# One buffer per PSUM bank, fillers only at the start, and a new step order in a fused attention and MLP kernel

## The chip, the cores and the metric

The kernel runs on one core of one Trainium2 chip. The time is device microseconds of one execution of the whole program; several executions are timed, and their median is compared. One more execution is recorded by the hardware profiler, and its span, from the first to the last instruction, is what the profile's shares refer to. The core has a matrix engine (TensorE, called PE, with its weight loads shown apart as PEld), three engines that work on whole tiles (VectorE or DVE, ScalarE or ACT, GpSimd or POOL), a fifth that here only issues transfers (SyncE or SP), and 16 DMA engines. Each engine takes its instructions strictly in the order in which the program gives them to it. PE's results go to PSUM, which has eight banks of 128 partitions by 512 fp32 values; DVE and ACT read them from there, POOL can't.

## The reference

Two stages follow one another: a linear attention with decay in blocks of 64 positions, and an MLP with the activation h + sin(alpha h)^2 / alpha. `q`, `k`, `v` are (4, 8, 768, 64), the MLP has 3072 tokens, 512 inputs and outputs and 2048 inner features.

```
for b in range(nb):
    intra = einsum('bhic,bhjc->bhij', qb, kb) * Dmask
    intra = einsum('bhij,bhjd->bhid', intra, vb)
    inter = einsum('bhid,bhde->bhie', qb * lam_pow, kv_state)
    out[:, :, sl] = intra + inter
    kv_state = lam_block * kv_state + einsum('bhsd,bhse->bhde', kb * rev_pow, vb)
x = out.transpose(0, 2, 1, 3).reshape(B * S, H * D)
h = x @ w_in
s = sin(alpha * h)
g = h + s * s / (alpha + 1e-09)
return (g @ w_out).astype(float32)
```

## The kernel before, in words

**Units.** The attention is cut into 24 units: 256 positions (two chunks of 128) of four heads of one batch element. For a unit `u`, SP loads three fp32 tiles (`ld{u}q`, `ld{u}k`, `ld{u}v`, line 694). `cq` and `ck` cast q and k to bf16 (line 706, on ACT, POOL or DVE), `sv` scales v by the decay (POOL, line 721). q and k are turned: for units 0 to 8 by PE (`tq`, `tk`, tile `pt`, line 729) with an eviction by ACT or DVE (`e0`, `e1`), for units 9 to 23 by a DMA that SP issues (`dt`, line 746). `sc` computes the scores into the tile `sp` (line 752), `mm` masks them (DVE, line 765). `kv` computes the unit's addition to the state (tile `kp`, in later units a part of `okv`, line 778); from it `bx` or `d0`, `d1` and `n0`, `n1` make the decayed state `kvbd` and what is carried on (DVE for units 3 to 7, else POOL, with an ACT copy `kva` ahead; lines 799 to 859). `in` and `io` multiply q by the state and the masked scores by v, both into `okv` (lines 864 and 875), and `oe` writes the unit's output, scaled, to the tile `xt` (DVE, line 894). From unit 8 on, `sc`, `kv` and the previous unit's `in` and `io` are one PE step, `step{u}`.

**Groups.** Four units make a group of 512 tokens; there are six. For each group, 16 steps `f1_g_f` multiply `xt` by 128 columns of `w_in` (four matmuls into the tile `hps`, line 911); ACT takes the sine (`sn`), ACT or POOL squares it (`sq`), DVE adds (`g`, into the tile `gall`). An `f1` step of a group needs all four of its units; only the first feature block of group 0 is done in two halves of two units each. Then four token tiles of 128 are multiplied by `w_out`, each in four quarters of four matmuls, `f2_g_m_j` (line 939), evicted by ACT (`ev`) and stored by SP (`out`). The weights are loaded and cast by POOL's DMA queue, `w_in` in four pieces `wi0` to `wi3` (256, 512, 512 and 768 columns), `w_out` in four equal ones `wo0` to `wo3`. A piece may be issued only after a named `sv` step (`WG` and `WH`, lines 538 and 539). The first load of unit 5 waits until the piece that holds feature block 4 of `w_out`, `wo1`, has landed (`GATES`, line 521), and SP takes its other instructions in order behind it.

**PSUM.** Four banks, `f0` to `f3`, hold `pt`, `kp`, `hps`, `ops` and a few tables, handed out by the planner; two banks hold `sp` and two hold `okv`. `bank()` (line 572) makes a new tile, with a name and shape of its own, under the bank's tag each time. The framework sets every semaphore wait; a tile under the same tag as an older one waits for all that used the older one.

**The order.** All steps are `Op` objects with a cost, the steps they come after, the buffers they take and give back, and a due time `vt`. `Plan.run` plays through the kernel with these costs: whenever an engine is free, it takes of the steps that are ready and whose buffers are free the one with the lowest due time. What comes out is only an order; each engine then runs its steps in it. `TUNE` adds a number to a step's due time and may pin the step to one engine. The due times without it are 32 per group and 8 per unit (`vt_unit`, line 1023, is 32 g - 40 + 8 r + u for unit u = 4 g + r up to unit 7); pieces of the weights have -700 plus their place among the eight.

**Fillers.** Nine matmuls of 512 columns and 60 of 256, `warm` with the tile `bz`, multiply constants into a free `f` bank and nobody reads them (lines 986 and 1012). In the plan each of the 60 takes 0.11 us and comes `FLAG` = 0.03 us or more after the one before. Their due times are 2,000,000 and up.

```
for i in range(NFILL):
    dop = add("warm", on("PE", 0.11), [dop], 2e6 + i, dummy, take=("f",), mode="n", lag=FLAG)
    dop.give, dop.part = ((dop, "f"),), 2
```

**What the plan knows of DMA.** `BEGIN` is how long after its issue a transfer starts, `FETCH` lists times at which transfers are slowed for `HOLD` = 1.5 us, `SHARE` is the rate that is left to them.

Of the kernel before, what the change touches and what calls it, by code (L numbers as in the profile page):

```python
# [12 lines left out]
FP32 = mybir.dt.float32  # L13
# [17 lines left out]
class Plan:  # L31
# [3 lines left out]
    BEGIN, LAND, DEPTH = {"SP": 0.4, "POOL": 2.4}, 1.3, 6  # L35
    HEAD = 0.75
    FETCH = (4.0, 14.5, 21.5, 27, 48, 56, 66.5, 76.5, 86, 98.5, 108.5, 121, 131.5, 142.5, 157)
    HOLD, SHARE = 1.5, 0.35
# [129 lines left out]
def kernel(  # L168
# [27 lines left out]
        "lam": (0.0, 'ACT'), "iden": (0.0, 'POOL'), "lamb": (0.0, 'PE'), "tabc": (0.0, 'DVE'),  # L196
        "tab1": (1.2, 'POOL'), "tabm": (852.8, 'DVE'), "tabi": (-21.2, 'POOL'),
        "tabd": (-499.1, 'POOL'), "tab2": (-428.0, 'DVE'), "tab0": (-2.1, 'PE'),
        "tab4": (-818.2, 'DVE'), "tab3": (-962.3, 'ACT'), "alq": (0.0, 'ACT'),
# [301 lines left out]
    WI = (256, 512, 512, 768)  # L501
    WO = (4, 4, 4, 4)
    HALVES = ()
    NWARM = 9
    NLAM = 2
    NFILL = 60
    FLAG = .03
    DMAT = {9, 10, 11, 12, 13, 14, 15, 16, 17, 18, 19, 20, 21, 22, 23}
    NH0 = 1
    H0 = 24  # L510
    NX = False
    UV = 0
    UE = 1
# [834 lines left out]
```

## Time and profile before

| | us |
|---|---|
| runs | 221.74, 220.77, 221.69 (median 221.69) |
| span of the profiled execution | 218.2 |
| PE busy, of the span | 211.9 |
| of it `f1` matmuls (`hps`, 388) | 91.9 |
| of it `f2` matmuls (`ops`, 368) | 83.1 |
| ACT, POOL, DVE busy | 141.3, 124.6, 121.0 |
| first `f1` half block starts | 19.02 |
| first `f1` block of group 1 starts | 57.62 |
| last matmul of `f2` ends, about | 214.1 |

The span is split over 40 slices of 5.45 us; in each, the page gives the busy share in tenths (9 is 90% or more) for each engine, the clock that PE was granted, and what DMA moved:

```profile
PE   8999999999999999999999999999999999999994
ACT  3454699656499664878968787476778695634220
POOL 7959599768989899999898755611101100001000
PEclk9999999999999999999999999999999999999999
GB/s 148 302 287 146 192 206 207 240 292 247 264 240 209 217 263 268 240 175 235 301 152 224 267 58 99 0 51 0 50 48 0 51 50 24 60 11 74 27 141 98
```

PE is shown as busy from the first slice to the last, POOL up to about 130 us, and DMA carries most of its bytes before 130 us. A busy figure doesn't tell work from filler. In the list of waits, each line has the engine and line that waited, what it waited for, and then the total in us, the number of times and the longest. In a timeline row come start, duration, engine, line, operation, tile written and tiles read, shape and count; in brackets the idle time ahead of it and what ended it ("issue" means that it waited for nothing that the profile shows). A row that stands for several instructions runs from the first one's start to the last one's end.

### The profile page before, as it was taken

What the parts mean: (1) busy time and instruction counts of PE and PEld (TensorE: products, weight loads), DVE (VectorE), ACT (ScalarE), POOL (GpSimd) and SP (SyncE); (2) the same over time, 40 slices, a digit from 0 to 9 for tenths busy, and PEclk for the clock granted to TensorE, in tenths of its full rate; (3) what the DMA queues carried; (4) which work ended last, traced back from release to release, by engine and by line L of the source; (5) the groups of instructions that cost most, each with busy time, mean ns of one, the idle gap of its engine ahead of it and who ended that gap; (6) DMA issues with size and microseconds to landing.
All of it is one profiled execution on the core that took longest, in us unless ns stands there. A gap on an engine that the chain in (4) does not pass through costs nothing.

```text
span 218.2 us, 5305 instructions
## 1 busy us (share of the span) xinstructions
PE 211.9 (97%) x2102; PEld 108.3 (50%) x2102; DVE 121.0 (55%) x176; ACT 141.3 (65%) x252; POOL 124.6 (57%) x209
## 2 busy tenths in 40 slices
PE   8999999999999999999999999999999999999994
PEld 3556644455544555545654545554444444444463
DVE  3457676457368974657794797975345451311100
ACT  3454699656499664878968787476778695634220
POOL 7959599768989899999898755611101100001000
PEclk9999999999999999999999999999999999999999
DMA  5999999898999999969999964020220221203164
GB/s 148 302 287 146 192 206 207 240 292 247 264 240 209 217 263 268 240 175 235 301 152 224 267 58 99 0 51 0 50 48 0 51 50 24 60 11 74 27 141 98
DMA packets 62139, 33.65 MB, mean 154 GB/s; under 512 B 17938, under 2 KB 59170, under 8 KB 62114
## 3 DMA queue, kind: packets, MB, share of 16 engines
q1 hardware_dynamic: 57776, 29.04, 59.5%
q0 software_dynamic: 4224, 4.19, 12.0%
q8 instruction: 16, 0.26, 0.5%
q10 hardware_dynamic: 114, 0.07, 0.1%
q14 instruction: 9, 0.07, 0.1%
HBM read 27.27 MB, written 6.29 MB: 154 GB/s over the span
## 4 chain that ended last, share of the span: by engine, by line
PE 90%; POOL 4%; issue 2%; ACT 1%; DVE 1%; POOLq 0%; ACTq 0%
PE hps L916 35%; PE ops L952 33%; PE bz L989 6%; PE sp L759 3%; PE okv L952 3%; PE okv L882 2%; PE pt L735 2%; PE okv L869 2%; PE okv L793 1%; POOL vb L725 1%; POOL kvs L859 1%; POOL qk L719 1%; PE kp L793 1%; DVE gall L935 1%; ACT s L923 1%
## 5 line engine op out<-in xcount | busy, mean ns | idle before, releaser
L935 DVE SCALAR_TENSOR_TENSOR gall<-s,r_sb,hps 128x512 bf16<-128x512 bf16 (+1 forms) x97 | 69.8, 740 | 63.7 <-ACT s L930 47.8
L916 PE MATMUL hps<-xt,w_in_sb 128*128 128x512 bf16 (+1 forms) x388 | 91.9, 377 | 1.4 <-DVE gall L935 0.8
L952 PE MATMUL ops<-w_out_sb,gall 128*128 128x512 bf16 (+1 forms) x368 | 83.1, 370 | 0.0
L923 ACT ACTIVATE s<-hps,alpha_sb 128x512 bf16<-128x512 f32 (+1 forms) x97 | 65.4, 679 | 25.9 <-PE hps L916 24.7
L952 PEld LDWEIGHTS <-gall 128*128 128x128 bf16 x400 | 38.5, 98 | 41.7
L916 PEld LDWEIGHTS <-w_in_sb 128*128 128x128 bf16 x388 | 36.5, 98 | 43.2 <-issue 2.6
L932 POOL TENSOR_TENSOR s<-s 128x512 bf16<-128x512 bf16 x21 | 21.9, 1041 | 51.9 <-ACT s L923 51.9
L930 ACT ACTIVATE s<-s 128x512 bf16<-128x512 bf16 (+1 forms) x76 | 46.6, 623 | 1.7
L767 DVE TENSOR_TENSOR sm<-sp,mask 128x1024 bf16<-128x1024 f32 x24 | 29.3, 1220 | 4.6 <-PE sp L759 4.5
L725 POOL TENSOR_TENSOR vb<-st_v,R 128x512 bf16<-128x512 f32 x24 | 25.0, 1045 | 2.5 <-DMA st_v<-in_v_dram 2.5
L958 ACT COPY ob<-ops 128x512 f32<-128x512 f32 x21 | 12.3, 584 | 20.2 <-PE ops L952 20.2
L821 POOL TENSOR_TENSOR kvbd<-kvx,LBD 128x256 bf16<-128x256 f32 x32 | 19.7, 614 | 2.5
L818 POOL TENSOR_TENSOR kvx<-kva,kvs 128x128 f32<-128x128 f32 x32 | 14.6, 456 | 7.8 <-ACT kva L803 7.7
L901 DVE TENSOR_TENSOR xt<-okv,ET 128x512 bf16<-128x512 f32 x24 | 16.5, 686 | 3.1 <-PE okv L882 2.8
L989 PE MATMUL bz<-const-bfloat16-1.0 128*128 128x256 bf16 (+1 forms) x69 | 16.4, 311 | 1.5 <-PEq L1332 0.8
L719 POOL CAST qk<-st_q 128x512 bf16<-128x512 f32 x19 | 11.5, 612 | 2.5 <-PE okv L793 2.5
L719 POOL CAST qk<-st_k 128x512 bf16<-128x512 f32 x17 | 10.4, 613 | 0.8 <-DMA st_k<-in_k_dram 0.8
L759 PE MATMUL sp<-qt 64*64 64x128 bf16 x384 | 10.0, 221 | 0.0
L882 PE MATMUL okv<-sm,vb 64*64 64x128 bf16 x384 | 9.7, 218 | 0.0
L859 POOL TENSOR_TENSOR kvs<-kvx,ET 128x128 f32<-128x128 f32 x24 | 9.4, 403 | 0.0
L803 ACT COPY kva<-okv 128x256 f32<-128x256 f32 (+1 forms) x16 | 5.0, 314 | 6.6 <-PE okv L793 6.4
L742 ACT COPY qt<-pt 128x512 bf16<-128x512 bf16 x9 | 5.2, 590 | 6.2 <-PE pt L735 6.2
(63 smaller groups left out, 110.7 us busy)
## 6 DMA issues: line engine op xcount, KB each, us to landing
st_q<-in_q_dram SPq DMA_DIRECT2D x24, 256.0 KB, 5.1
st_k<-in_k_dram SPq DMA_DIRECT2D x24, 256.0 KB, 5.3
st_v<-in_v_dram SPq DMA_DIRECT2D x24, 256.0 KB, 5.0
out_dram<-ob SPq DMA_DIRECT2D x46, 128.0 KB, 2.5
w_out_sb<-in_moe_w_out_dram POOLq DMA_DIRECT2D x4, 512.0 KB, 11.9
w_in_sb<-in_moe_w_in_dram POOLq DMA_DIRECT2D x2, 512.0 KB, 6.4
w_in_sb<-in_moe_w_in_dram POOLq DMA_DIRECT2D x1, 768.0 KB, 9.6
w_in_sb<-in_moe_w_in_dram POOLq DMA_DIRECT2D x1, 256.0 KB, 6.4
```

The costliest lines, as they stand in the source:

```text
L719: ENGINE[op.eng].tensor_copy(out=o, in_=i)
L725: ENGINE[op.eng].tensor_tensor(out=T[u, "vb"][:], in0=T[u, "v"][:].rearrange("p h two e -> p two h e"), in1=R[:, :, hs].unsqueeze(3).to_br ...
L759: nc.tensor.matmul(out=T[u, "sp"][half[c], hd, par, hp, :], lhsT=QT[half[hd], 1, par, hp, half[c]], rhs=QT[half[hd], 0, :, hp, half[c]], s ...
L767: V.tensor_tensor(out=T[u, "sm"][:].rearrange("p hd par hp i -> p (hd par) hp i"), in0=T[u, "sp"][:].rearrange("p hd par hp i -> p (hd par ...
L821: G.tensor_tensor(out=bd[:], in0=X.unsqueeze(2).to_broadcast([P, 2, 2, D]), in1=LBD[:, hs, :].unsqueeze(3).to_broadcast([P, 2, 2, D]), op= ...
L916: op.ins = nc.tensor.matmul(out=op.tile[:, cols], lhsT=w_in_sb[:, c, f * P:(f + 1) * P], rhs=xt[g][:, c].rearrange("p b c i -> p (b c i)") ...
L923: A.activation(out=op.tile[:, cols], in_=mm.tile[:, cols], func=ACTF.Sin, scale=alpha_sb[:, f:f + 1])
L930: A.activation(out=op.tile[:, cols], in_=s1, func=ACTF.Square)
L932: ENGINE[op.eng].tensor_tensor(out=op.tile[:, cols], in0=s1, in1=s1, op=ALU.mult)
L935: V.scalar_tensor_tensor(out=gall[g][:, f, cols], in0=sq.tile[:, cols], scalar=r_sb[:, f:f + 1], in1=mm.tile[:, cols], op0=ALU.mult, op1=A ...
L952: op.ins = nc.tensor.matmul(out=first.tile[:, cols], lhsT=gall[g][:, f, m * P:(m + 1) * P], rhs=w_out_sb[:, f, cols], start=(f == 0), stop ...
L989: nc.tensor.matmul(out=bz[:, :w], lhsT=nc.const_aps.tensor(1.0, [P, P], BF16), rhs=nc.const_aps.tensor(1.0, [P, w], BF16), start=True, sto ...
```

## The change

Four things change. `bank()` makes one tile per `f` bank for the whole kernel, when the bank is first used, and returns a view of it in the shape and type asked for. Fillers are planned as before, with `FLAG` 0.2 instead of 0.03, and those that the plan starts at 40 us or later are not emitted. Three of the planner's DMA figures are new. Every number in `TUNE` is new (949 entries each), and most pins are gone: before, all but 21 entries named an engine, after, 46 do, among them the evictions, casts and squares of the early units and groups.

```diff
-    BEGIN, LAND, DEPTH = {"SP": 0.4, "POOL": 2.4}, 1.3, 6
+    BEGIN, LAND, DEPTH = {"SP": 0.4, "POOL": 1.9}, 1.3, 6
     HEAD = 0.75
-    FETCH = (4.0, 14.5, 21.5, 27, 48, 56, 66.5, 76.5, 86, 98.5, 108.5, 121, 131.5, 142.5, 157)
-    HOLD, SHARE = 1.5, 0.35
+    FETCH = (4.0, 21.5, 48, 56, 66.5, 76.5, 86, 98.5, 108.5, 121, 131.5, 142.5, 157)
+    HOLD, SHARE = 1.5, 0.6
...
-        "n12": (-186.7, 'POOL'), "in2": (2000055.6, 'PE'), "io2": (2000064.6, 'PE'),
-        "oe2": (-8.6, 'DVE'), "cq3": (24.5, 'POOL'), "ck3": (0.0, None), "sv3": (-5.1, 'POOL'),
...
-        "sc3": (2000052.1, 'PE'), "kv3": (2000051.2, 'PE'), "mm3": (-71.1, 'DVE'),
...
-        "n13": (-0.3, 'POOL'), "in3": (0.0, 'PE'), "io3": (2000059.7, 'PE'), "oe3": (-891.7, 'DVE'),
...
-        "in4": (-69.2, 'PE'), "io4": (29.2, 'PE'), "oe4": (0.0, 'DVE'), "cq5": (70.3, 'ACT'),
-        "ck5": (-287.2, 'ACT'), "sv5": (118.3, 'POOL'), "tq5": (-92.8, 'PE'), "e05": (68.8, None),
...
-        "oe5": (5.3, 'DVE'), "cq6": (0.0, 'ACT'), "ck6": (32.1, 'POOL'), "sv6": (-90.1, 'POOL'),
...
-        "oe7": (96.4, 'DVE'), "wi0": (-221.9, 'POOL'), "wi1": (679.4, 'POOL'), "wi2": (-215.8, 'POOL'),
-        "wi3": (-216.7, 'POOL'), "wo0": (15.7, 'POOL'), "wo1": (641.9, 'POOL'), "wo2": (651.7, 'POOL'),
-        "wo3": (233.0, 'POOL'), "f1_0_0_0": (2000064.1, 'PE'), "sn_0_0_0": (7.9, 'ACT'),
...
+        "mm0": (-4766.324, None), "kc0": (1911.615, None), "bx0": (844.407, None),
...
+        "mm1": (-4066.408, None), "kc1": (-5167.704, None), "bx1": (838.066, None),
...
+        "mm2": (1856.667, None), "kc2": (2302.111, None), "bx2": (820.657, None),
...
+        "in2": (-1077.365, None), "io2": (-1259.15, None), "oe2": (-4839.027, None),
+        "cq3": (751.21, 'POOL'), "ck3": (-5210.075, None), "sv3": (893.615, None),
...
+        "e13": (1876.351, 'DVE'), "sc3": (-488.995, None), "kv3": (-1262.126, None),
...
+        "in3": (-1478.921, None), "io3": (-1403.597, None), "oe3": (1832.935, None),
...
+        "cq5": (1870.301, 'POOL'), "ck5": (2371.136, 'POOL'), "sv5": (-2403.737, None),
...
+        "cq6": (1946.789, 'POOL'), "ck6": (1946.633, 'POOL'), "sv6": (-3742.543, None),
...
+        "wi0": (2661.259, None), "wi1": (1530.709, None), "wi2": (1496.33, None),
+        "wi3": (1451.672, None), "wo0": (1312.938, None), "wo1": (1410.162, None),
+        "wo2": (2654.22, None), "wo3": (3033.606, None), "f1_0_0_0": (-1298.656, None),
...
-    FLAG = .03
+    FLAG = .2
...
+    fbank = {}
+
     def bank(op, kind, shape, dt, name, n=0):
-        return ps.tile(shape, dt, name=name, tag=op.bank[kind][n])
+        tag = op.bank[kind][n]
+        if tag not in fbank:
+            fbank[tag] = ps.tile([P, 512], FP32, name=tag, tag=tag)
+        x = fbank[tag][:]
+        if dt == BF16:
+            x = x.bitcast(BF16)
+        size = 1
+        for d in shape[1:]:
+            size *= d
+        x = x[:shape[0], :size]
+        if len(shape) > 2:
+            names = [f"a{i}" for i in range(len(shape) - 1)]
+            x = x.rearrange(f"p ({' '.join(names)}) -> p {' '.join(names)}",
+                            **dict(zip(names, shape[1:])))
+        return x
...
     for op in plan.run():
-        op.emit(op)
+        if op.name != "warm" or op.start < 40:
+            op.emit(op)
```

More of the change, by code (lines that the diff above doesn't have):

```diff
@@ L195 @@
     TUNE = {
[L196 to L199, printed above, removed]
[285 rows of a table removed]
+        "lam": (2856.137, None), "iden": (1880.546, None), "lamb": (-281.166, None),
+        "tabc": (2673.263, None), "tab1": (1875.154, None), "tabm": (2662.034, None),
+        "tabi": (1694.732, None), "tabd": (1331.443, None), "tab2": (2217.537, None),
+        "tab0": (-885.153, None), "tab4": (1820.232, None), "tab3": (1895.814, None),
+        "alq": (2855.914, None), "alpha": (-874.852, None), "alphav": (2226.001, None),
[376 rows of a table added]
     }
```

639 rows, old and new, of the table TUNE are left out of this document.

## The prediction

> **What bounds the kernel now.** First the page's head and the filler group, for the engine that sets the time:
>
> ```profile
> span 218.2 us, 5305 instructions
> PE 211.9 (97%) x2102; PEld 108.3 (50%) x2102; DVE 121.0 (55%) x176; ACT 141.3 (65%) x252; POOL 124.6 (57%) x209
> ...
> L989 PE MATMUL bz<-const-bfloat16-1.0 128*128 128x256 bf16 (+1 forms) x69 | 16.4, 311 | 1.5 <-PEq L1332 0.8
> ```
>
> PE is busy 97% of the span, but 16.4 us of that are 69 matmuls that nobody reads (`bz`). So PE's share says nothing yet: the question is where filler stands in the way of work. Second, the stretches (time, then busy us and instructions of PE, PEld, DVE, ACT, POOL, then granted clock, DMA share, GB/s):
>
> ```profile
> 6.00:17.00 11.00, 10.38 (x186) 6.06 (x184) 5.56 (x9) 6.02 (x15) 8.53 (x12) 1.00 1.20 290
> 17.00:19.00 2.00, 2.00 (x47) 1.48 (x45) 1.46 (x3) 0.00 (x0) 1.98 (x3) 1.00 0.44 52
> 19.00:38.00 19.00, 18.37 (x171) 9.25 (x171) 13.04 (x21) 15.32 (x29) 16.09 (x27) 1.00 1.21 201
> 38.00:62.00 24.00, 24.00 (x267) 12.13 (x266) 12.76 (x20) 14.27 (x29) 18.93 (x32) 1.00 0.98 265
> 62.00:66.00 4.00, 3.07 (x17) 1.43 (x16) 3.03 (x6) 3.60 (x6) 4.00 (x6) 1.00 1.08 211
> 66.00:200.00 134.00, 133.90 (x1312) 67.19 (x1312) 81.39 (x107) 95.29 (x164) 70.55 (x115) 1.00 0.61 125
> ```
>
> From 38 us on PE lacks 0.93 us (62 to 66) and 0.10 us (66 to 200); the chain of waits is PE alone there. That stretch can only move as a block, by the time at which the first f1 blocks begin. Filler lies in 0 to 25 us (62 pieces) and at the end (7). So third, PE and PEld just ahead of the last unit that f1's first group needs, with the DVE row that released it:
>
> ```profile
> 20.02 1.91 PE L989 MATMUL bz<-const-bfloat16-1.0 128*128 128x256 bf16 x6
> 20.19 0.41 DVE L835 TENSOR_TENSOR kvbd<-kp,LBD 128x256 bf16<-128x256 f32 x1
> 20.36 0.10 PEld L989 LDWEIGHTS <-const-bfloat16-1.0 128*128 128x128 bf16 x1 [0.23 <-issue]
> 20.69 0.10 PEld L989 LDWEIGHTS <-const-bfloat16-1.0 128*128 128x128 bf16 x1 [0.23 <-issue]
> ...
> 21.66 0.20 PEld L869 LDWEIGHTS <-kvbd 128*128 128x128 bf16 x2 [0.23 <-issue]
> 21.77 0.27 PE L869 MATMUL okv<-qt,kvbd 128*128 128x128 bf16 x2
> ```
>
> Its operand `kvbd` is there at 20.60, the mask at 20.28, and yet `okv` starts at 21.77: it stands behind six fillers that come 0.325 us apart, each after a 0.23 us pause. Where several banks are free they follow at 0.11 us (17.11: five in 0.72 us). The pause is PE waiting for its own last filler, since a new buffer in the same bank waits for all users of the old one. Fourth, the weight loads on POOL and SP's wait for one of them:
>
> ```profile
> 21.52 1.54 POOL L688 DMA_DIRECT2D w_out_sb<-in_moe_w_out_dram  x2
> 26.48 1.54 POOL L688 DMA_DIRECT2D w_out_sb<-in_moe_w_out_dram  x2
> ...
> SPq L699 <- DMA w_out_sb<-in_moe_w_out_dram: 24.7, 1, 24.7
> ```
>
> **The change part by part.** The sum is made against this execution's 218.2 us; the median of the runs, 221.69, lies 3.5 us above it, and I carry those 3.5 us unchanged.
>
> A. *One buffer per bank.* No release any more between a filler and what follows in its bank: writer after writer on one engine needs no wait. Six fillers from 20.02 then end at 20.02 + 6 x 0.11 = 20.68, and `okv` runs at about 20.8 instead of 21.77: 1.0 us. The same pause of 0.21 us stands ahead of unit 3's `kp` at 19.76, which feeds this `kvbd`: 0.2 us. And unit 2's `sp` ran at 15.30 behind three such fillers and a `kp`, 0.2 us later than at 0.11 us a filler; its mask, and unit 3's behind it on DVE, move with it. Taken: -1.4 us. Bounds: 0 (another engine ends there instead) and -3.9 us (all that the waits list as PEld L989 on issue). The trace's row is 0.325 us a filler; the Trainium skill, PSUM — Partial Sum Buffer, Engine vs sequencer instructions, says that matmuls start and complete in program order, so that their writes land in issue order. By that rule no wait is owed and the spacing is 0.11 us; by the row alone, were the wait kept, part A would be 0.
>
> B. *Due times against fillers.* In the old table some two dozen early PE steps (`kv3`, `sc3`, `io2`, `io3` among them) carry about +2,000,050, behind most fillers' 2,000,000 + i; in the new one none does, so a ready step always goes first. On the path: unit 2's `okv` at 17.98 could follow the read of its bank, ended at 17.58, by 0.1; a filler and a 0.16 us pause are between. -0.3 us, bounds 0 and -0.6 (unit 3's `sp`, ready at 17.91, ran at 18.55).
> FLAG 0.03 to 0.2 spaces fillers at 0.31 us in the plan instead of 0.14; they cost 0.11 where PE is idle: 0.
>
> C. *POOL's queue, first loads.* The second w_in load, issued at 16.60, leaves DMA at 52 GB/s from 17 to 19 us, against 201 after: 2.0 x (1 - 52/201) = 1.5 us of stream. By due times it keeps its neighbours (behind the first three `kvbd`, ahead of `sv3`), so the hole shrinks only as POOL's waits for `kva` (1.07 and 0.59 us) do. Bounds 0 to -1.5; taken 0, as that load lands at 16.60 + 6.4 = 23.0, and its first reader, the block at 25.39, finds it landed even 1.7 us earlier.
>
> D. *Does the head start get through 38 to 62?* PE has no idle time there, but f1's second group (57.62) needs units 4 to 7, whose loads wait for `wo1` to land: 37.56. Old due times (-700 + place + table) put `wo1` third (-680, -460, -53, -42 for wo0, wo3, wo1, wo2); new ones (617, 715, 1960, 2340) put it second. Issued with the pair at 21.52, it lands 11.9 us (median) after some 22.3: 34.2, or 3.4 us sooner. So A and B's 1.7 us pass: 0 lost; bound +1.7 (all lost). `wo2` and `wo3` come later for it; f2's first two quarters for four tiles, 8 x 0.86 = 6.9 us, cover that.
>
> E. *Stalls in runs of f1.* PE idles 0.35 us at 30 to 35, 0.93 at 62 to 66, 0.10 after, because ACT needs 0.69 + 0.63 us a block when it squares too, against PE's 0.86. A new order deals these runs anew: between -1.4 and, if twelve blocks instead of five run in a row, 0.93 x 7/5 = +1.3 us. Taken -0.3, an estimate: 0.51 of the 0.93 us is one wait for a turn's bank that DVE empties at 65.63, and nothing ties that step to this run; some of it should go.
>
> F. *Fillers after planned 40 us dropped.* Seven at 213.96 to 214.90, beside the last eviction (DVE, 214.22 to 214.64) and the last sends (214.67): 0, at most -0.2.
>
> G. *Casts.* `cq5`, `ck5` and `cq6` go from ACT (43.19, 43.70, 44.69) to POOL: 3 x 0.61 = 1.8 us, inside POOL's 24.00 - 18.93 = 5.1 us idle in 38 to 62: 0. With that cover gone it is +1.8, and what is late is `kvbd`, then `xt`, then f1's second group.
>
> H. *The planner's DMA figures* decide only where steps are put, but PE takes them in that order. The rows bear out the new ones: DMA moves 324 and 334 GB/s from 14 to 16 us and 207 from 27 to 28 (205 two slices before), so the two dropped dips aren't there; from 326 to 182 at 4 to 5 us is a share of 0.56, near 0.6. Taken 0. Were the old ones true, weights would come 0.5 + 2 x 1.5 x 0.65 = 2.4 us after their readers' places: bound +2.4, 222.1.
>
> Sum: -1.4 - 0.3 - 0.3 = -2.0: span 216.2, time **219.7**; own range 218.3 to 220.8.
>
> **The rivals.**
> 1. *The start is drawn together further.* Unit 3's `k` lands near 8.57 + 5.3 = 13.9; cast 0.62, turn 0.39, eviction 0.42, scores 0.42, mask 1.22, output 0.42, `xt` 0.69 and six handovers of 0.2 make 19.3, and it is at 23.13 now. With the DMA hole closed weights follow. -3.8: 217.9. For it: POOL waits 1.07 and 0.59 us for ACT's `kva` there, and holds the second w_in load behind it. Against: POOL is busy 8.53 of 11 us in this stretch. Chance 0.12.
> 2. *A wait takes its place at 57 us*: units 4 to 7 come no sooner, A and B are paid back, E stays: 221.4. For it: POOL heads the chain of waits from 51 to 61 us. Chance 0.12.
> 3. *Slower: POOL becomes the bound in 38 to 66.* It takes G's three casts and is 4.00 of 4 us busy at 62 to 66 already. If its idle time before the last `kvbd` of units 4 to 7 falls below 1.8 us, f1's second group is 1.8 us late and the early gain is lost in the same wait: 220.0, time 223.5, and one more square there (1.04) 224.5. Against: its waits for ACT and DMA make up the 5.1 us, and loads come sooner. Chance 0.28.
> 4. *The shared buffer doesn't free the fillers*: A is 0: 221.1. Chance 0.05.
> 5. *The clock falls.* Thinner fillers leave PE idle between steps. The first four wide ones took 1.86 us, 0.465 each, against 0.216 for an f1 matmul of the same size later, so the slow clock costs half of its time; 3.2 us of it are 1.6 us: 221.3. Against: granted clock 1.00 in every stretch, although between 20 and 22 us PE streamed only a third of the time. Chance 0.05. (The Trainium skill, TensorE: Matmul & The Clock Gate, Why this matters for your kernels, warns of PE-idle gaps above about 3 us; no run here shows one.)
>
> **How the numbers follow.** Forecast 0.38, rivals as given. About 0.5%, 1.1 us, is what the measurement can tell, so faster is below 220.6 and slower above 222.8. Faster: 0.36 + 0.12 + 0.02 = 0.50. Same: 0.02 + 0.09 + 0.07 = 0.18. Slower: 0.28 with 0.04 from rivals 2 to 5 and E's upper end: 0.32. The range 216.8 to 224.2 leaves out the better part of rival 1 and rival 3's extra squares.
>
> **What would show it.** A: fillers 0.11 us apart also in one bank, no 0.23 us pauses on issue. B: first wide f1 block about 1.7 us before its 23.8. D: SP's loads for unit 5 near 34, f1's second group before 57.6. E: PE idle after 30 us below 1.4. F: last eviction and sends as far from the end as now, 4 us. I am wrong if PE idles more than 2 us between 38 and 66, if POOL's casts end there just ahead of the waiting step, or if the clock leaves 1.00.

## The result, and the profile after

The changed kernel took 219.19 us, median of 14 runs (216.77 to 221.72), against 221.31 (220.71 to 221.87) for the kernel before on the same chip: ratio 0.9879, interval 0.9855 to 0.9903. Three of the 14 runs (220.11, 221.07 and 221.72) are of a slower state, and the ratios, here and below, leave such runs out, so they aren't the quotients of the medians (without the three the median is 218.66). The prediction said 219.7. The head of the page and the filler group, as before:

```profile
span 216.9 us, 5246 instructions
PE 207.5 (96%) x2065; PEld 105.9 (49%) x2065; DVE 120.7 (56%) x177; ACT 138.0 (64%) x248; POOL 126.4 (58%) x212
...
L1097 PE MATMUL f<-const-bfloat16-1.0 128*128 128x256 bf16 (+1 forms) x32 | 9.8, 393 | 0.8 <-PEq L1441 0.8
```

All tiles of the four banks are now called `f`; the fillers are told by their operand, the constant 1.0. There are 32 instead of 69, and they take 9.8 us instead of 16.4. PE is again busy from end to end by share, which again says little. The stretches (time, then busy us and instructions of PE, PEld, DVE, ACT, POOL, then clock, DMA share, GB/s):

```profile
17.00:19.00 2.00, 1.38 (x32) 0.99 (x27) 1.90 (x3) 1.10 (x2) 1.45 (x2) 1.00 1.14 185
19.00:38.00 19.00, 18.46 (x154) 9.03 (x152) 12.44 (x20) 15.18 (x29) 18.18 (x31) 1.00 1.21 203
38.00:62.00 24.00, 23.74 (x338) 12.45 (x339) 14.49 (x22) 13.55 (x28) 21.09 (x33) 1.00 1.11 270
62.00:66.00 4.00, 4.00 (x48) 1.97 (x40) 3.79 (x6) 3.76 (x8) 3.71 (x8) 1.00 0.97 276
66.00:90.00 24.00, 21.98 (x288) 11.35 (x288) 14.57 (x20) 15.66 (x28) 22.21 (x40) 1.00 1.08 239
66.00:200.00 134.00, 131.98 (x1227) 65.96 (x1227) 77.34 (x102) 93.10 (x161) 67.41 (x109) 1.00 0.57 122
```

Three things differ. The hole in the DMA stream at 17 to 19 us is gone (185 GB/s for 52). PE's idle time at 62 to 66 (0.93 us) is gone too. But between 66 and 90 PE now idles 2.0 us, where it idled 0.1 before. The clock is 1.00 in all six stretches. PE's timeline at the start, and where group 1 begins:

```profile
12.58 0.49 PE L1097 MATMUL f<-const-bfloat16-1.0 128*128 128x256 bf16 x3
...
15.55 0.49 PE L1097 MATMUL f<-const-bfloat16-1.0 128*128 128x256 bf16 x3
...
18.61 0.61 PE L1024 MATMUL f<-xt,w_in_sb 128*128 128x256 bf16 x4 [0.62 <-DMA w_in_sb<-in_moe_w_in_dram]
...
20.90 1.46 PE L1024 MATMUL f<-xt,w_in_sb 128*128 128x256 bf16 x8
22.31 1.89 PE L1024 MATMUL f<-xt,w_in_sb 128*128 128x512 bf16 x8
...
55.19 1.89 PE L1024 MATMUL f<-xt,w_in_sb 128*128 128x512 bf16 x8
```

In the kernel before, the row that stands for the one at 20.90 was:

```profile
23.22 1.46 PE L916 MATMUL hps<-xt,w_in_sb 128*128 128x256 bf16 x8
```

Three fillers last 0.49 us from the first start to the last end, where one alone lasts 0.28: they come 0.11 us apart, without a pause. The rows at 20.90 and 23.22 run from narrow into wide matmuls: behind four narrow ones, 0.11 us each, the first wide block begins at 21.34, 2.3 us earlier than the 23.66 of before (the prediction read 23.8). The first half block at 18.61 now waits for the first `w_in` load, which POOL issues at 11.44 instead of 8.81; in the kernel before it stood behind a filler, 1.4 us after its second `xt` was written (17.58). The first block of group 1 begins at 55.19, 2.43 us earlier, and the early gain is whole up to there. From there to the end of the span it is 161.7 us, against 218.2 - 57.62 = 160.6 before: 1.1 us are given back, in the stretch from 66 to 90. Each profile is one execution: in seven more, of the experiments below, that have the same instructions up to there, group 1 begins at 54.65 to 55.97. What ends the longest wait there, on PE, and SP's transfers ahead of it:

```profile
88.76 0.42 PE L867 MATMUL sp<-qt 64*64 64x128 bf16 x16 [1.38 <-DMA qt<-qk]
```

```profile
71.09 3.13 SPq L856 DMA_TRANSPOSE qt<-qk  x1
74.27 1.88 SPq L1088 DMA_DIRECT2D out_dram<-ob  x2
...
82.29 0.69 SPq L807 DMA_DIRECT2D st_q<-in_q_dram  x1
83.08 2.17 SPq L1088 DMA_DIRECT2D out_dram<-ob  x2
85.35 2.70 SPq L856 DMA_TRANSPOSE qt<-qk  x2
```

Between the turn of unit 12 (71.09) and those of units 13 and 14 (85.35) SP issues two pairs of stores and eight loads. The scores of unit 13 wait for the turn.

### The profile page after: what moved, and what is told of

Its sections match the earlier page's. It is cut to its first block, busy times and chain, and to the rows that moved or that the text cites. A ratio compares the mean times of both kernels' runs of the same rounds, so it can differ in the third digit from the quotient of the medians.

```text
span 216.9 us, 5246 instructions
## 1 busy us (share of the span) xinstructions
PE 207.5 (96%) x2065; PEld 105.9 (49%) x2065; DVE 120.7 (56%) x177; ACT 138.0 (64%) x248; POOL 126.4 (58%) x212
## 4 chain that ended last, share of the span: by engine, by line
PE 69%; DMA 16%; POOL 7%; ACT 2%; issue 2%; DVE 1%; SPq 1%; POOLq 0%; ACTq 0%
PE f L1024 30%; PE f L1060 29%; DMA st_q<-in_q_dram 5%; DMA qt<-qk 5%; DMA w_in_sb<-in_moe_w_in_dram 3%; PE f L1097 3%; DMA st_v<-in_v_dram 2%; PE sp L867 2%; PE okv L990 2%; POOL s L1040 2%; ACT s L1031 1%; POOL qk L827 1%; POOL vb L833 1%; PE okv L977 1%; POOL kvbd L929 1%
## 5 line engine op out<-in xcount | busy, mean ns | idle before, releaser
L1043 DVE SCALAR_TENSOR_TENSOR gall<-s,r_sb,f 128x512 bf16<-128x512 bf16 (+1 forms) x97 | 69.5, 740 | 56.2 <-ACT s L1038 44.3
L1024 PE MATMUL f<-xt,w_in_sb 128*128 128x512 bf16 (+1 forms) x388 | 91.6, 377 | 1.7 <-DVE gall L1043 0.9
L1031 ACT ACTIVATE s<-f,alpha_sb 128x512 bf16<-128x512 f32 (+1 forms) x97 | 64.8, 679 | 31.0 <-PE f L1024 26.7
L1060 PE MATMUL f<-w_out_sb,gall 128*128 128x512 bf16 (+1 forms) x368 | 82.9, 370 | 0.0
L1040 POOL TENSOR_TENSOR s<-s 128x512 bf16<-128x512 bf16 (+1 forms) x22 | 22.4, 1020 | 37.7 <-ACT s L1031 35.4
L1066 ACT COPY ob<-f 128x512 f32<-128x512 f32 x21 | 12.3, 584 | 22.1 <-PE f L1060 22.1
L827 POOL CAST qk<-st_k 128x512 bf16<-128x512 f32 x19 | 11.6, 611 | 0.4 <-DMA st_k<-in_k_dram 0.2
L1097 PE MATMUL f<-const-bfloat16-1.0 128*128 128x256 bf16 (+1 forms) x32 | 9.8, 393 | 0.8 <-PEq L1441 0.8
L850 ACT COPY qt<-f 128x512 bf16<-128x512 bf16 x8 | 4.7, 588 | 6.9 <-PE f L843 6.9
L867 PEld LDWEIGHTS <-qt 64*64 64x64 bf16 x384 | 6.4, 108 | 4.9 <-DMA qt<-qk 1.9
```

The costliest lines, as they stand in the source:

```text
L827: ENGINE[op.eng].tensor_copy(out=o, in_=i)
L867: nc.tensor.matmul(out=T[u, "sp"][half[c], hd, par, hp, :], lhsT=QT[half[hd], 1, par, hp, half[c]], rhs=QT[half[hd], 0, :, hp, half[c]], s ...
L1024: op.ins = nc.tensor.matmul(out=op.tile[:, cols], lhsT=w_in_sb[:, c, f * P:(f + 1) * P], rhs=xt[g][:, c].rearrange("p b c i -> p (b c i)") ...
L1031: A.activation(out=op.tile[:, cols], in_=mm.tile[:, cols], func=ACTF.Sin, scale=alpha_sb[:, f:f + 1])
L1040: ENGINE[op.eng].tensor_tensor(out=op.tile[:, cols], in0=s1, in1=s1, op=ALU.mult)
L1043: V.scalar_tensor_tensor(out=gall[g][:, f, cols], in0=sq.tile[:, cols], scalar=r_sb[:, f:f + 1], in1=mm.tile[:, cols], op0=ALU.mult, op1=A ...
```

## The experiments

Medians and ratios are against runs of the kernel before on the same chip; they can be compared within one group.

| run | us | before | ratio, interval |
|---|---|---|---|
| the change again | 218.69 | 221.52 | 0.986, 0.982 to 0.989 |
| views only | 218.60 | 221.52 | 0.988, 0.986 to 0.991 |
| order only | 219.52 | 221.52 | 0.989, 0.986 to 0.992 |
| early stores on ACT | 224.76 | 221.52 | 1.015, 1.011 to 1.018 |
| three turns ahead | 219.01 | 221.41 | 0.993, 0.989 to 0.996 |
| no narrow fillers | 218.96 | 221.41 | 0.989, 0.986 to 0.993 |
| all fillers | 219.52 | 221.41 | 0.993, 0.990 to 0.996 |
| casts on ACT | 218.81 | 221.41 | 0.987, 0.982 to 0.992 |
| two turns ahead | 218.10 | 220.80 | 0.986, 0.983 to 0.989 |
| two turns, square on ACT | 217.75 | 220.80 | 0.985, 0.982 to 0.989 |
| the change, third time | 218.70 | 221.71 | 0.987, 0.984 to 0.990 |
| two turns, square on ACT, again | 217.28 | 221.71 | 0.981, 0.979 to 0.984 |

### The change again, and its two halves

The changed kernel as it is:

> The changed kernel itself, beside the variants below. All theories: ratio to the kernel before near 0.988, PE idle about 2 us between 66 and 90 us, waiting for a turned tile.

It came out alike: span 216.5, group 1's first block at 55.13, PE idle for 1.97 us at 66 to 90. Then each half of the change alone. The kernel before with only the new `bank()`:

```diff
+    fbank = {}
     def bank(op, kind, shape, dt, name, n=0):
-        return ps.tile(shape, dt, name=name, tag=op.bank[kind][n])
+        tag = op.bank[kind][n]
+        if tag not in fbank:
+            fbank[tag] = ps.tile([P, 512], FP32, name=tag, tag=tag)
...
```

> The kernel before with one buffer per bank, nothing else: old step order, old fillers. Theory A (a filler's successor in its bank no longer waits): fillers 0.11 us apart in one bank, first wide f1 block 1.4 us sooner than 23.8, and the whole 1.4 us reach the end: ratio 0.994. Rival (the head start is paid back): the first wide block is 1.4 us sooner all the same, but w_out's second piece is still issued third and lands near 37.6, so f1's second group starts at 57 or later and the ratio is 0.998 to 1.000. Rival (views don't free the fillers): they stay 0.325 us apart, ratio 1.000.

and the changed kernel with the old `bank()`:

```diff
-        tag = op.bank[kind][n]
-        if tag not in fbank:
...
+        return ps.tile(shape, dt, name=name, tag=op.bank[kind][n])
```

> The changed kernel with a new tile for each use of a bank, as before; new order, fillers as changed. Theory A: pauses of 0.23 us behind fillers return; with some ten fewer fillers in the start than before they cost 0.7 to 1.4 us: ratio 0.991 to 0.994. Rival (the order alone makes the gain): ratio 0.988.

PE's timeline of the run with views only, at the place that the prediction took from the kernel before (six fillers, then unit 3's `okv`):

```profile
19.09 0.84 PE L1005 MATMUL f<-const-bfloat16-1.0 128*128 128x256 bf16 x6
19.77 0.27 PE L885 MATMUL okv<-qt,kvbd 128*128 128x128 bf16 x2
...
21.22 1.46 PE L932 MATMUL f<-xt,w_in_sb 128*128 128x256 bf16 x7
```

The six fillers take 0.84 us instead of 1.91. `okv` follows at 19.77 instead of 21.77, and the first wide block at 21.66, 2.0 us earlier (the last row's count lacks one of eight matmuls, which the trace didn't keep). SP's loads for unit 5 start at 35.78 (37.61 before), although `wo1` is still third among the loads of `w_out`: its queue began earlier, since the second `w_in` load was issued at 15.24 instead of 16.60. Group 1 begins at 55.69, 1.93 us earlier; from there to the end it is 216.2 - 55.69 = 160.5 us, as before. So the buffers alone give as much as the whole change.

With the order alone the pauses are back (PE's timeline of that run; 0.60 us for three fillers instead of 0.49, and for two instead of 0.38), and yet the first wide block stands at about 22.0, 1.7 us earlier than before, and group 1 at 55.51, 2.1 us earlier:

```profile
15.81 0.60 PE L1081 MATMUL bz<-const-bfloat16-1.0 128*128 128x256 bf16 x3
...
19.10 0.60 PE L1081 MATMUL bz<-const-bfloat16-1.0 128*128 128x256 bf16 x2
```

Fewer fillers are left that could stand in the way (32 for 69). The two halves remove the same delay by different means, and so don't add up: 1.9 and 2.1 us at group 1 alone, 2.4 together. (Group 1's start differs by up to 1.3 us between executions, so which of the three is largest isn't shown; that 4.0 isn't reached is.) And the order alone shows the stall of the changed kernel, with 2.87 us idle at 66 to 90; from group 1 to the end it is 218.0 - 55.51 = 162.5 us. The stall belongs to the order.

### The stall at 66 to 90 us

The first try gave the stores of groups 0 to 2 to ACT, so that no store stands ahead of a turn on SP:

```diff
-            SY.dma_start(out=rows[par], in_=ev.tile[par * D:(par + 1) * D, :])
+            (A if g < 3 else SY).dma_start(out=rows[par], in_=ev.tile[par * D:(par + 1) * D, :])
```

> The changed kernel with the output stores of the first three groups issued by ACT instead of SP. Theory (the turns by DMA stand behind stores on SP): the turn issued at 85.35 behind a store of 2.2 us goes out near 83.1, the wait of 1.38 us for it at 88.76 goes, ratio about 0.983. Rival (the turns wait for their inputs or a free slot): they go out at the same time, ratio 0.988. Rival (issuing holds ACT up): 24 issues of about 0.5 us each delay ACT's evictions, ratio above 0.990.

PE's idle time at 66 to 90 fell to 0.42 us, but the kernel became slower than before. ACT's timeline of this run tells why (56.31 is an eviction, 59.43 a pair of stores, 61.41 a sine), with two lines of its waits from 55 to 90 us:

```profile
56.31 0.59 ACT L1066 COPY ob<-f 128x512 f32<-128x512 f32 x1 [4.23 <-DMA out_dram<-ob]
...
59.43 1.88 ACTq L1088 DMA_DIRECT2D out_dram<-ob  x2
61.41 0.69 ACT L1031 ACTIVATE s<-f,alpha_sb 128x512 bf16<-128x512 f32 x1 [3.26 <-DMA qt<-qk]
```

```profile
ACT ob L1066 <- DMA out_dram<-ob: 4.2, 1, 4.2
ACT s L1031 <- DMA qt<-qk: 3.3, 1, 3.3
```

Issuing the two stores took ACT 0.54 and 0.48 us. The rest of the 3.26 us ahead of the sine is waiting: by the profile the stores, at about 59.4 and 60.8, each came after a turned tile had landed. The eviction had waited 4.2 us for a store to land. So ACT's own work stood behind transfers. DVE and PE stood behind the sine, and PE had nothing to do from 60.5 to 63.7. PE's timeline and the same run's stretches show what follows (columns of the stretches as above):

```profile
63.72 3.54 PE L1024 MATMUL f<-xt,w_in_sb 128*128 128x512 bf16 x8 [3.19 <-DVE gall L1043]
```

```profile
61.00:62.00 1.00, 0.00 (x0) 0.00 (x0) 0.00 (x0) 0.59 (x2) 0.00 (x0) 1.00 1.11 356
62.00:63.00 1.00, 0.00 (x0) 0.00 (x0) 0.08 (x1) 1.00 (x4) 0.48 (x2) 1.00 1.03 309
63.00:64.00 1.00, 0.28 (x1) 0.10 (x1) 1.00 (x2) 1.00 (x3) 0.59 (x1) 0.85 1.08 318
64.00:65.00 1.00, 1.00 (x4) 0.35 (x3) 0.73 (x2) 0.56 (x2) 0.88 (x1) 0.50 1.08 325
65.00:66.00 1.00, 1.00 (x4) 0.41 (x3) 1.00 (x2) 0.32 (x1) 1.00 (x2) 0.50 1.18 328
```

After an idle gap of 3.2 us the granted clock is 0.50 until 67 us, and eight wide matmuls take 3.54 us instead of 1.89.

Next, the turns were issued earlier instead. The list of all steps is changed after the plan has been made:

```diff
+    order = plan.run()
+    for turn, load_ in (("dt12", "ld15q"), ("dt13", "ld15v"), ("dt14", "ld18q")):
+        op = next(o for o in order if o.name == turn)
+        order.remove(op)
+        order.insert(next(i for i, o in enumerate(order) if o.name == load_), op)
```

> The changed kernel with three of SP's instructions moved ahead, all else as it is: the DMA turns of units 12, 13 and 14 are issued two, six and two instructions earlier, ahead of loads of units 15 to 18 and of one pair of stores. Theory (the new stall at 66 to 90 us is the new order's: turns stand on SP behind loads and stores that nobody needs yet): PE's idle time at 66 to 90 falls from 2.0 to below 0.8 us, the turn of unit 13 is issued near 76 instead of 85.3, and the saving reaches the end: span 215.0 to 215.6, median 217.2 to 217.8, 1.0 to 1.5 us below the changed kernel. Rival (the turns are slow because DMA is full there, and the displaced loads become late in their turn): idle time only moves to another wait or another place between 66 and 110 us, and the time is within 0.5 us of the changed kernel, 218.2 to 219.2.

The rival was right. The idle time at 66 to 90 fell to 0.85 us, but at 90 to 110 1.88 us came anew. The rows that lead there are, on POOL of this run, a cast of unit 15's q and a square, and on DVE the step that reads the square:

```profile
76.75 0.61 POOL L827 CAST qk<-st_q 128x512 bf16<-128x512 f32 x1 [2.13 <-issue]
...
93.09 1.04 POOL L1040 TENSOR_TENSOR s<-s 128x512 bf16<-128x512 bf16 x1
...
94.17 2.06 DVE L1043 SCALAR_TENSOR_TENSOR gall<-s,r_sb,f 128x512 bf16<-128x512 bf16 x3 [4.18 <-POOL s L1040]
```

In the changed kernel that cast starts at 75.31 and that square at 91.65. Unit 15's q load was issued 1.7 us later, behind unit 12's turn; its cast came 1.44 us later, and from there on POOL works without a gap, so that the square is 1.44 us late as well. Only units 13 and 14 were moved next:

```diff
-    for turn, load_ in (("dt12", "ld15q"), ("dt13", "ld15v"), ("dt14", "ld18q")):
+    for turn, load_ in (("dt13", "ld15v"), ("dt14", "ld18q")):
```

> The changed kernel with only the DMA turns of units 13 and 14 issued earlier on SP (ahead of unit 15's v load and of unit 18's q load); unit 12's turn stays behind unit 15's q load. Theory (POOL, always busy from 75 us on, is the next bound: in the run with three turns moved, unit 15's q load was issued 1.7 us later, its cast on POOL started at 76.75 instead of 75.31, and everything behind it on POOL, among it the square that DVE then waited 4.2 us for, was 1.44 us later too): now that cast starts at 75.3 again, the square starts near 91.65, PE is idle 0.6 to 1.0 us at 66 to 90 and 0.3 to 0.6 us at 90 to 110, 1.0 us less in all than in the changed kernel; span 215.6 to 216.2, median 217.5 to 218.2. Rival (the moved turns themselves, not the q load, make POOL late, or the stall moves on whatever is done): PE idles 1.9 us or more at 66 to 110 again, median 218.4 to 219.2.

and besides them the square given to ACT:

```diff
+        if op.name == "sq_2_4_None":
+            op.eng = "ACT"
```

> As the run with the turns of units 13 and 14 moved, and the square of group 2's feature block 4, at about 91.7 on POOL, done by ACT at its place in the order. Theory (POOL's late square is what PE then waits for at 92 to 95 us): DVE's wait for POOL's square goes, PE is idle 0.2 us or less at 90 to 110, and POOL's work behind it comes 1.0 us earlier; span 0.3 to 0.6 us below that run, median 217.0 to 217.8, the fastest of all so far. Rival (ACT is then late instead, or PE is held by something else there): PE idle at 90 to 110 stays at 0.3 us or more and the time is within 0.3 us of that run.

With two turns moved PE idles 0.05 us at 86 to 90 (1.38 in the changed kernel) and 0.16 at 90 to 110: no new stall. What is left at 66 to 90, 1.55 us, was expected at 0.6 to 1.0; 1.03 of it is one wait at 71.25 for a square of group 1 on POOL, itself behind a cast that waited 1.0 us for unit 12's q. This wait differs from run to run (0 to 1.0 us). The square on ACT gained nothing that shows: DVE waits 1.7 us for ACT's square where it waited 1.7 us for POOL's, and PE idles 0.16 us at 90 to 110 either way, as in the changed kernel run again. Beside the changed kernel on one chip:

> The changed kernel once more, only so that it stands on one chip beside the next run. Both theories expect 218.0 to 219.2, and PE idle 1.7 to 2.2 us at 66 to 110.

> The kernel with the turns of units 13 and 14 moved ahead on SP and group 2's square 4 on ACT, beside the changed kernel on one chip. Theory (PE's idle time at 66 to 110 was on the path to the end): PE idles 0.5 to 1.0 us there, and the median is 0.9 to 1.4 us below that of the changed kernel. Rival (PE's idle time there is paid for elsewhere, or the two medians of earlier runs differed by their chips only): within 0.4 us of it.

The same stretch, 66 to 90 us, first of the changed kernel and then of the mended one:

```profile
66.00:90.00 24.00, 21.80 (x286) 11.37 (x289) 14.56 (x20) 16.11 (x29) 22.18 (x41) 1.00 1.19 236
```

```profile
66.00:90.00 24.00, 22.88 (x289) 11.83 (x288) 15.75 (x21) 16.08 (x29) 22.89 (x41) 1.00 1.09 241
```

PE's idle time is 2.2 against 1.1 us here, and the medians are 218.70 against 217.28, 1.4 us apart. This version is faster than both kernels. PE's idle time there varies between executions: 1.3 to 2.2 us in the six profiles with the changed order and buffers and no turn or store moved, 0.6 to 1.6 in the three with two turns moved. Its waits for turned tiles alone are clearer: 1.4 to 1.8 us in the three profiles of the changed kernel, 0 to 0.2 in these three. From group 1's first block to the end it is 161.4 to 161.7 us in the former and 159.9 to 160.8 in the latter, about the 160.6 of the kernel before. So idle time in this stretch lies on the path to the end. The two profiles beside one another differ by another 1.0 us ahead of group 1 (55.97 against 54.99), before the first moved turn: the start varies, and in them the first half block waited 1.0 and 0.3 us for `w_in`.

### Fillers and casts

The emission rule was changed both ways, first to the nine wide fillers only, then to all of them:

```diff
-        if op.name != "warm" or op.start < 40:
+        if op.name != "warm" or op.part == 1:
```

> The changed kernel without its 23 narrow fillers; the nine wide ones at the beginning stay. Theory A (with one buffer per bank a filler costs no more than its own 0.11 us, and the plan puts it where PE is idle anyway): the first wide f1 block stays at 21.3 to 21.5 us, or comes up to 0.2 us earlier, and the time is within 0.4 us of the changed kernel. Theory of the clock (rival 5): PE is idle for more than 3 us somewhere between 9 and 19 us, the granted clock falls below 1.00 there, and the first wide block comes 0.5 to 1.6 us later, time 219.2 to 220.5. If fillers were still in the way: 0.5 us or more earlier.

The clock stayed at 1.00 from 13 to 15 us in the profiled execution, though PE was busy for only 1.26 of the 2 us. The first wide block began at 21.32, as expected; the second came late, at 24.04. Two rows of the start (`pt`, the turn on PE) and the one of the second block:

```profile
9.69 0.63 PE L843 MATMUL f<-iden,qk 128*128 128x128 bf16 x4
...
10.91 0.38 PE L843 MATMUL f<-iden,qk 128*128 128x128 bf16 x4 [0.23 <-DVE qt L852]
...
24.04 1.25 PE L1024 MATMUL f<-xt,w_in_sb 128*128 128x512 bf16 x5 [1.58 <-DMA w_in_sb<-in_moe_w_in_dram]
```

The second block waited for the second `w_in` load. The two rows of `pt` show what the granted clock in the stretches doesn't (it reads 1.00 there too): PE is slow at first, here until some moment between the two. In the changed kernel's profile four matmuls of `pt` take 0.63 us at 6.16 and 0.39 at 9.18, in that of the kernel before 0.38 already at 4.96. The moment differs between executions of the same instructions (with three turns moved, 0.39 at 4.87); whether the narrow fillers bring it forward isn't shown. The median, 218.96, lies within 0.4 us of the 218.7 of the changed kernel on two other chips. So the narrow fillers cost nothing that shows, and leaving them out costs nothing that shows either.

> The changed kernel with every filler of its plan emitted, 37 more than now: one just ahead of the last matmuls, 36 behind them. Step F says 0, at most 0.2 us: the last eviction and the last sends run beside them, so the span is 216.5 to 217.1 and the time within 0.3 us of the changed kernel. Rival: the 36 fillers, 0.11 us each, last 4.0 us behind the last matmul and end after the last sends, so the span is 0.3 us or more longer.

The rival was right here. The last fillers and the copy ahead of the last sends, in the timeline of this run:

```profile
212.42 4.20 PE L1097 MATMUL f<-const-bfloat16-1.0 128*128 128x256 bf16 x36
212.68 0.42 DVE L1074 COPY ob<-f 128x256 f32<-128x256 f32 x1 [11.89 <-DMA out_dram<-ob]
```

In the kernel before, and in the changed one, the span ends 4.0 us after that copy begins. Here it would be 216.7, but the fillers end at 216.62, and the span at 217.6: 0.9 us later. Then the three casts back on ACT, at their places:

```diff
+        if op.name in ("cq5", "ck5", "cq6"):
+            op.eng = "ACT"
```

> The changed kernel with the casts of units 5 (q and k) and 6 (q) given back from POOL to ACT, at the same places in the order: step G undone. Step G says 0 (POOL keeps over 2 us idle between 38 and 62): POOL's busy time at 38 to 62 falls by 1.8 us from 21.1, the first f1 block of group 1 stays within 0.3 us of 55.2, and the time within 0.4 us of the changed kernel. Rival 3 (POOL sets the end of that stretch): the first block of group 1 comes 0.5 to 1.8 us earlier. ACT as the bound there: it comes later by 0.5 us or more.

POOL's busy time at 38 to 62 fell by 1.85 us, from 21.09 to 19.24; group 1 began at 55.70, 0.5 us later than the 55.2 named, and the time was the same, 218.81. Most of the 0.5 us is the start of this execution, whose first half block waited 0.91 us for `w_in` and ran 0.4 us later. Relieving POOL there gains nothing: it doesn't set the end of that stretch.

## Why the prediction was right, and where not

The forecast of 219.7 lies 0.5 us above the median. Its mechanism, fillers that held the first units, is right. Two of its sizes are wrong, in opposite directions, and that the sum comes so near is in part luck: A and B gave 0.7 us more than taken, E was 1.3 us worse.

- **A, taken -1.4.** Right in kind: one buffer per bank takes the pauses away, and with views alone they are gone. That was the outcome by the rule of the Trainium skill that the prediction cited (PSUM — Partial Sum Buffer, Engine vs sequencer instructions); the trace agrees, at 0.11 us. The size was too small: alone it moves the first wide block by 2.0 us and group 1 by 1.9. The six fillers ahead of unit 3's `okv` give 1.07 of the 2.0, as counted. What lies ahead of them gives 0.9, for the 0.4 counted: unit 2's `kp` runs at 13.80 instead of 15.05, and POOL's waits for `kva`, 1.07 and 0.59 us, shrink to 0.18. POOL's queue comes earlier with them, and issues the second `w_in` load 1.4 us sooner.
- **B, taken -0.3.** The order alone, with 32 fillers instead of 69, moves group 1 by 2.1 us; how much of it is due times, `FLAG` or fewer fillers wasn't taken apart. It is no term to add to A: both are ways to the same 2 us. Together 2.4, against 1.7 predicted.
- **C, taken 0.** The hole in DMA closed. What the step missed is the first `w_in` load, issued 2.6 us later than before; the first half block now waits 0.2 to 1.0 us for it in the three profiles of the changed kernel. This fits the wider spread of its runs (216.8 to 219.7 in the 11 that the ratio uses, against 220.7 to 221.9), but wasn't tried, and the moment at which PE comes to full speed varies too.
- **D, 0 lost.** The number held: unit 5's loads came at 33.75 for the 34.2 given, and the gain went through. But `wo1`'s new place wasn't needed for a head start of 1.9 us, as the run with views only shows.
- **E, taken -0.3: the step that failed.** The stall at 62 to 66 went, as said, but the new order made one of 2.0 us at 66 to 90. PE's idle time from 30 to 200 us rose from 1.38 to 2.34 us: +0.96 where -0.3 was taken, inside the step's bounds but with the other sign. The step looked for stalls of ACT in runs of `f1`. It was SP's order instead: turns behind loads and stores that nobody needs yet. The size it had on the path is the 1.1 us from group 1 to the end.
- **F, 0.** The count was wrong: with `FLAG` 0.2 the new plan puts 36 fillers behind the last matmul, not seven. The time was right for the kernels compared, but the new plan needs the rule; without it the end comes 0.9 us later.
- **G, 0.** Right: POOL had cover for the three casts. **H, 0:** nothing in the traces speaks against it, and nothing tested it alone.
- **The 3.5 us above the span** were not overhead. The timed executions have spans of their own, and their times lie about 1.75 us above them; the profiled execution of the kernel before, at 218.2, was shorter than the timed ones (219.0 to 220.1 by that difference). It is one of the fastest: its PE came to full speed early, but that this is the reason isn't shown. So the spans differ by only 1.3 us (218.2 and 216.9), the medians by 2.1 to 3.0.
- **Rivals.** Rival 2 fell: nothing is paid back at 57 us. Rival 3 fell at its place, 38 to 66; but POOL without a gap after 75 us did set what moving three turns was worth. Rival 4 fell with the views. Rival 5 fell for the kernel from 17 us on, where the clock holds; whether the thinner fillers lengthen PE's slow start isn't shown. Rival 1, a start drawn together by 3.8 us, came about by 0.7 of the 2.1 us that it adds to A and B.

## What to carry to other kernels

Work that only keeps an engine busy must be free of releases: a buffer that is made anew at each use can make the engine wait for itself, and one buffer with views removes that. When a plan is made anew, follow every in-order queue past the stretch that the change is meant for, the one that issues transfers above all; look at what stands ahead of each transfer that somebody waits for. Two remedies for one delay don't add up; try each alone. A profile is one execution: before a difference of under 1 us is explained, take a second one.

## What the runs showed of the hardware

- A matmul into a bank whose last tile nobody reads came 0.325 us after the one before when it waited for its release, and 0.11 without.
- Between its start and its end the kernel lost the full clock only after PE had been idle for 3.2 us: 0.50 for some 3 us. Gaps up to 1.9 us and a share of 1.26 of 2 us left it at 1.00. The prediction cited the Trainium skill (TensorE: Matmul & The Clock Gate, Why this matters for your kernels) for gaps above about 3 us. This case's trace agrees.
- At the start PE is slow, until a moment that differs between executions: four matmuls of `pt` still took 0.63 us at 6.16 in the changed kernel, and 0.39 at 4.87 with three turns moved.
- Issuing one store took ACT about 0.5 us, but a pair took 1.88 us, as the second came only after a turn had landed. Issuing the turn at 71.09 took SP 3.13 us.
